# Memory attention with two dense stages on one core: exp(phi) kept row-major, the first batch's keys and values in wide products, tokens left in permuted order

## The chip, the cores and the metric

The kernel runs on one core of a Trainium2 chip. The metric is the device time of one execution in microseconds. Engines are named as in the profile: PE is TensorE's matmul stream, PEld its weight loads, DVE VectorE, ACT ScalarE, POOL GpSimd, SP the engine whose queue issues the loads and stores.

## The reference

Attention runs through 32 memory slots per head (4 batches, 8 heads, 576 tokens, width 64). Its output, 2304 tokens by 512, goes through a leaky two-matrix stage and then through four experts that are mixed by normalised probabilities.

```python
a = np.exp(phi - np.max(phi, axis=2, keepdims=True))
a = a / (np.sum(a, axis=2, keepdims=True) + 1e-09)
k_m = np.einsum('bhsm,bhsd->bhmd', a, k)
v_m = np.einsum('bhsm,bhsd->bhmd', a, v)
scores = scale * np.matmul(q, k_m.transpose(0, 1, 3, 2))
attn = softmax(scores)                       # over the 32 slots
x = rows(np.matmul(attn, v_m))               # (2304, 512)
h = x @ w_in;  x = np.maximum(0.01 * h, h) @ w_out      # w_in, w_out are float64
p = domain_probs / domain_probs.sum(-1, keepdims=True)
out = sum(p[:, e:e+1] * (np.maximum(x @ w1[e], 0) @ w2[e]) for e in range(4))
```

Here axis 2 of phi is the sequence: the maximum and the sum run over the 576 tokens of a head.

## The kernel before, in words

**Layout.** A load of q, k, v or phi of one batch puts two heads on the 128 partitions, 64 partitions to a head; a partition holds nine consecutive rows (tokens) of its head, and four such pairs of heads lie side by side. So token number s is row s mod 9 of partition s // 9. `LT` is 9, `HG` is 4, `NGB` is 2.

**Attention of one batch** (`att_batch`), in its stages: the maximum over the rows in a partition (line 510), a transpose, the maximum over partitions (515), a broadcast back (517, 520), the subtraction (522) and exp (525), all in place in `pl`; a transpose of q in 32x32 blocks (528, `qT`); z, the sums of exp(phi), by matmuls with `ones` (540); the products of exp(phi) with k and v (548), in tiles of 64 by 32 of the array; division by z (574, in `kv`); transposes of the keys to `kb` and the values to `vt` (590, 586); then for each half s of the sequence the scores (610), a block transpose (618), softmax (625 to 638), another transpose (641) and a split of the result into a rounded and a rest part (332, 335: `ah`, `al`). The scores read `qT` in token order, so that neighbouring columns of the moving operand lie 64 elements apart. In batch 0 the k product and the v product are separate, in the other batches they are one.

**First dense stage** (`y_pair`, `moe1_step`). A step is for one batch, half and chunk of 128 hidden units; batch 0 comes first, its first half with chunks 0 to 5, then its second half. A step has six products that make the hidden units (884) and four groups of three that multiply by w_out (951, 952, 953); y pairs (900) put v_m and w_in together. The float64 weights come as pieces of raw words that ACT, DVE and POOL convert (782 to 803); four early pieces use the room of `X2` and `X3`, where q and k of batch 1 are to go. A load into `X1` (v of batch 1) and those pieces lie interleaved in the same stretch of memory.

**What sets the order.** Every operation is handed to a planner (`Plan.op`) with an engine, a cost, a due time and the keys that it reads and writes; `Plan.issue` lists them by cost and due time and so fixes the order on each engine before anything runs. The engines then run in that order, each waiting for what it needs. In the first 50 us of its own reckoning the planner also puts in idle matmuls (line 453) where PE would have nothing to do. The DMA queue of SP is in order as well: a load that has to wait holds up all loads behind it, and a load waits for the landing of the one eight before it.

Of the kernel before, what the change touches and what calls it, by code (L numbers as in the profile page):

```python
# [31 lines left out]
class Plan:  # L32
# [13 lines left out]
    WARM, PART, IDLE, SHORT = (3.0, 50.0), 0.5, 0.22, 0.5  # L46
# [129 lines left out]
def kernel(  # L176
# [42 lines left out]
    PERIOD, LEAD, EACH, LAST = 32.0, 34.0, 3.0, -7.0  # L219
# [150 lines left out]

    def load_probs(t):
        nc.sync.dma_start(out=pr[:, t, :], in_=moe2_domain_probs[t * P:(t + 1) * P, :])
# [71 lines left out]
    def tile_(shape):  # L444
        n = 1
        for size in shape:
            n *= size
        return place("att", new("att", n), *shape)
    ident = tile_([P])

    def idle(bank):

        nc.tensor.matmul(psum[:, bank, 0:P], lhsT=ident, rhs=ident, start=True, stop=True)  # L453
# [3 lines left out]
    pl = [tile_([HG, LT * M]) for i in range(2)]  # L457
    mr = tile_([P])
# [28 lines left out]
    def load(what, b, due):  # L487

        if what == "p":
            plan.op("SP", 1.8, due, lambda: nc.sync.dma_start(  # L490
                out=pl[b % 2], in_=phi[b].rearrange("h s m -> (h s m)").rearrange("(h p w) -> p h w", h=HG, p=P)),
                writes=[f"pl{b % 2}"])
            return
        src, name = {"k": k, "v": v, "q": q}[what], HOME[what][b]
        plan.op("SP", 3.5, due, lambda: nc.sync.dma_start(
            out=home(name), in_=src[b].rearrange("h s d -> (h s d)").rearrange("(h p w) -> p h w", h=HG, p=P)),
            writes=[name])

    def att_batch(b):


        a = pl[b % 2].rearrange("p h (r m) -> p h r m", r=LT)
        nmx, rz = [small[nm][b % 2] for nm in ("nmx", "rz")]
        qn = HOME["q"][b]
        ka = f"pl{b % 2}"
# [4 lines left out]
        op("DVE", 1.25, due, lambda: nc.vector.tensor_reduce(  # L510
            out=mr.rearrange("p (h m) -> p h m", h=HG), in_=a.rearrange("p h r m -> p h m r"), axis=AX.X, op=ALU.max),
           [ka], ["mr"])
        pm = Banks(psum, 1)
        op("PE", 0.13, due, lambda: nc.tensor.transpose(pm[0:P], mr, ident), ["mr", "ident"], [pm])
# [5 lines left out]
        op("PE", 0.13, due, lambda: nc.tensor.transpose(pb[0:P], mb.rearrange("p g t -> p (g t)"), ident),  # L520
           ["mb", "ident"], [pb])
        op("DVE", 1.3, due, lambda: nc.vector.tensor_tensor(
            out=a, in0=a, in1=pb[0:P].rearrange("p (h m) -> p h m", h=HG).unsqueeze(2).to_broadcast([P, HG, LT, M]),
            op=ALU.subtract), [pb], [ka])
        op("ACT", 1.2, due, lambda: nc.scalar.activation(out=pl[b % 2], in_=pl[b % 2], func=AF.Exp), [], [ka])
# [5 lines left out]
        for names in (("k",), ("v",)) if b == 0 else (("k", "v"),):  # L531
            due = yield
            pkv = Banks(psum, 2)
# [3 lines left out]
            def fn(pkv=pkv, src=src, n=len(names), first="k" in names):  # L537
                for r in range(LT * first):
                    for h in range(HG):
                        nc.tensor.matmul(  # L540
                            pkv[2 * D:2 * D + NGB][h * M:(h + 1) * M], lhsT=a[:, h, r], rhs=ones,
                            start=(r == 0), stop=(r == LT - 1),
                        )
                for r in range(LT):
                    for h in range(HG):
                        for g in range(NGB):
                            gs = slice(g * D, (g + 1) * D)
                            nc.tensor.matmul(  # L548
                                pkv[g * 512:g * 512 + n * D][h * M:(h + 1) * M].rearrange("p (i d) -> p i d", i=n),
                                lhsT=a[gs, h, r],  # L550
                                rhs=src[gs, :, h, r * D:(r + 1) * D],
                                start=(r == 0),
                                stop=(r == LT - 1),
                            )
            op("PE", 0.9 + 0.6 * len(names), due, fn, [ka, "ones"] + [HOME[nm][b] for nm in names], [pkv])

            def fn(pkv=pkv):
                nc.vector.tensor_scalar_add(rz, pkv[2 * D:2 * D + NGB], 1e-9)
                nc.vector.reciprocal(rz, rz)
# [3 lines left out]
            for g in range(NGB):  # L563

                def fn(e, g=g, pkv=pkv, n=len(names), lo=lo):
                    for i in range(n):
                        if n == 2 and lo:
                            out, in_ = kv[:, g, 1 - i], pkv[g * 512 + i * D:g * 512 + (i + 1) * D]
                        elif i:
                            break  # L570
                        else:
                            out, in_ = kv[:, g, lo:lo + n].rearrange("p i d -> p (i d)"), pkv[g * 512:g * 512 + n * D]
                        if e == "ACT":
                            nc.scalar.mul(out, in_, rz[:, g:g + 1])
                        else:
                            nc.vector.tensor_scalar_mul(out, in_, rz[:, g:g + 1])
                op("ACT", 0.3, due, fn, [pkv, f"rz{b % 2}"], [f"kv{g}{nm}" for nm in names], also=("DVE", 0.3))

            for nm in names:
# [12 lines left out]
                op("PE", 0.16 * n, due, fn, [f"kv{g}{nm}" for g in range(NGB)] + ["ident"], [pk])  # L592
# [7 lines left out]
        for s in range(2):  # L600
# [16 lines left out]
            op("PE", 0.9, due, fn, ["qT", "kb"], [ps], [f"at{s}"])  # L617
# [36 lines left out]
        ("q", 0): ["q2"], ("v", 0): ["p2", "v1"],  # L654
        ("k", 1): ["p3", "k2", "v2"],
        ("q", 2): ["q3"], ("k", 2): ["k3", "v3"],
# [12 lines left out]
    loads(["p0", "k0", "v0", "q0", "p1", "k1", "q1"])  # L669
# [17 lines left out]
    for t_ in range(NTILE):  # L687
        plan.op("SP", 0.6, 150.0 + 4 * t_, partial(load_probs, t_), [], ["probs"])
# [10 lines left out]
    def raw_piece(src, due, after, alone=False):  # L699
# [18 lines left out]
        plan.op("SP", 0.8 * size / 512, due - FETCH, partial(nc.sync.dma_start, out=t, in_=src), after, [rk])  # L718
# [391 lines left out]
    def second_products(t, n):  # L1110
# [4 lines left out]
        for i in range(2 * TPB):  # L1115
# [80 lines left out]
```

## Time and profile before

| what | us |
|---|---|
| median of 3 runs (lowest, highest) | 1178.17 (1177.49, 1180.21) |
| the profiled execution | 1179.85 |
| its span, first to last instruction | 1177.9 |
| PE busy in the span | 1146.6 |
| DVE, ACT, POOL busy | 681.9, 436.0, 98.9 |

The profile is of one execution. A busy PE isn't PE at its peak, and the clock that TensorE was granted stands beside it in the page. The span and the execution's time differ by what lies around the first and the last instruction.

### The profile page before, as it was taken

What the parts mean: (1) busy time and instruction counts of PE and PEld (TensorE: products, weight loads), DVE (VectorE), ACT (ScalarE), POOL (GpSimd) and SP (SyncE); (2) the same over time, 40 slices, a digit from 0 to 9 for tenths busy, and PEclk for the clock granted to TensorE, in tenths of its full rate; (3) what the DMA queues carried; (4) which work ended last, traced back from release to release, by engine and by line L of the source; (5) the groups of instructions that cost most, each with busy time, mean ns of one, the idle gap of its engine ahead of it and who ended that gap; (6) DMA issues with size and microseconds to landing.
All of it is one profiled execution on the core that took longest, in us unless ns stands there. A gap on an engine that the chain in (4) does not pass through costs nothing.

```text
span 1177.9 us, 18878 instructions
## 1 busy us (share of the span) xinstructions
PE 1146.6 (97%) x7852; PEld 1033.5 (88%) x7852; DVE 681.9 (58%) x1238; ACT 436.0 (37%) x889; POOL 98.9 (8%) x101
## 2 busy tenths in 40 slices
PE   6689999999999999999999999999999999999998
PEld 5468789999999999899989899999999899999997
DVE  3568546863343778767676753445476654454643
ACT  2555437853343544433332421322224123222220
POOL 1352104530000000000000000000000000000000
PEclk8879999999999999999999999999999999999999
DMA  8471302410000228554553563444444644444401
GB/s 322 158 252 44 96 2 89 150 69 1 1 19 1 98 91 318 180 188 187 197 197 143 171 204 144 161 161 161 159 143 139 193 144 161 161 161 161 146 34 53
DMA packets 55957, 160.88 MB, mean 137 GB/s; under 512 B 5441, under 2 KB 24897, under 8 KB 49729
## 3 DMA queue, kind: packets, MB, share of 16 engines
q1 hardware_dynamic: 51264, 100.97, 24.5%
q0 software_dynamic: 4608, 58.72, 14.1%
q8 instruction: 61, 1.00, 0.3%
q14 instruction: 24, 0.19, 0.0%
HBM read 125.60 MB, written 34.08 MB: 136 GB/s over the span
## 4 chain that ended last, share of the span: by engine, by line
PE 95%; DVE 1%; DMA 1%; issue 1%; ACT 1%; POOL 0%; POOLq 0%; SPq 0%; DVEq 0%
PE psum L1059 30%; PE psum L1129 11%; PE psum L1128 11%; PE psum L1127 11%; PE psum L884 9%; PE psum L951 6%; PE psum L953 6%; PE psum L952 6%; PE psum L610 2%; PE psum L900 1%; PE psum L548 1%; PE psum L453 1%; DMA exact<-in_q_dram 1%; DMA exact<-in_v_dram 0%; DVE exact L794 0%
## 5 line engine op out<-in xcount | busy, mean ns | idle before, releaser
L1068 DVE TENSOR_TENSOR exact<-psum,exact 128x384 f32<-128x384 f32 x336 | 184.1, 556 | 272.1 <-PE psum L1059 270.2
L1075 ACT ACTIVATE rounded<-exact 128x384 fp32r<-128x384 f32 x192 | 100.8, 525 | 284.4 <-DVE exact L1068 282.6
L335 DVE TENSOR_TENSOR rounded<-exact,rounded 128x288 fp32r<-128x288 f32 (+3 forms) x225 | 124.8, 571 | 100.3 <-ACT rounded L332 99.2
L1129 PE MATMUL psum<-late,rounded 128*128 128x512 f32 x384 | 150.7, 392 | 0.0
L1128 PE MATMUL psum<-late,rounded 128*128 128x512 f32 x384 | 150.5, 392 | 0.0
L1127 PE MATMUL psum<-late,rounded 128*128 128x512 f32 x384 | 149.3, 389 | 0.0
L1059 PE MATMUL psum<-rounded 128*128 128x384 f32 x768 | 143.2, 335 | 0.0
L1059 PEld LDWEIGHTS psum<-rounded 128*128 128x128 f32 x768 | 134.7, 188 | 2.4 <-DVE exact L1068 0.3
L884 PE MATMUL psum<-rounded 128*128 128x288 f32 x768 | 125.4, 300 | 2.2 <-DVE rounded L335 2.2
L332 ACT CAST rounded<-exact 128x288 fp32r<-128x288 f32 (+3 forms) x239 | 114.8, 501 | 19.8 <-POOL exact L802 5.8
L951 PE MATMUL psum<-rounded 128*128 128x288 f32 x384 | 116.1, 302 | 6.0 <-POOL rounded L335 5.6
L884 PEld LDWEIGHTS psum<-rounded 128*128 128x128 f32 x768 | 110.1, 191 | 9.2 <-issue 5.6
L952 PE MATMUL psum<-rounded 128*128 128x288 f32 x384 | 113.6, 296 | 0.0
L953 PE MATMUL psum<-rounded 128*128 128x288 f32 x384 | 113.6, 296 | 0.0
L1059 PE MATMUL psum<-late,rounded 128*128 128x384 f32 x576 | 109.9, 336 | 0.0
L1079 DVE SCALAR_TENSOR_TENSOR rounded<-exact,rounded 128x384 fp32r<-128x384 f32 x192 | 98.8, 551 | 13.0 <-ACT rounded L1075 13.0
L1059 PEld LDWEIGHTS psum<-late,rounded 128*128 128x128 f32 x576 | 102.0, 188 | 4.0 <-ACT exact L1090 0.2
L939 ACT ACTIVATE exact<-psum 128x288 f32<-128x288 f32 x128 | 53.4, 417 | 137.5 <-PE psum L884 134.6
L1090 ACT COPY exact<-psum 128x384 f32<-128x384 f32 x48 | 23.0, 480 | 198.1 <-PE psum L1059 198.1
L951 PEld LDWEIGHTS psum<-rounded 128*128 128x128 f32 x384 | 72.8, 190 | 18.7 <-issue 10.7
L1129 PEld LDWEIGHTS psum<-late,rounded 128*128 128x128 f32 x384 | 72.0, 188 | 15.1
L1128 PEld LDWEIGHTS psum<-late,rounded 128*128 128x128 f32 x384 | 72.0, 188 | 13.4
(103 smaller groups left out, 1696.1 us busy)
## 6 DMA issues: line engine op xcount, KB each, us to landing
rounded<-kept POOLq DMA_DIRECT2D x22, 1792.0 KB, 7.6
exact<-in_moe_w_dram SPq DMA_DIRECT2D x64, 512.0 KB, 5.0
kept<-rounded SPq DMA_DIRECT2D x10, 1792.0 KB, 6.7
w<-kept POOLq DMA_DIRECT2D x10, 1792.0 KB, 7.6
kept<-w SPq DMA_DIRECT2D x6, 1792.0 KB, 6.4
exact<-in_moe_w_in_dram SPq DMA_DIRECT2D x16, 512.0 KB, 5.5
exact<-in_moe_w_out_dram SPq DMA_DIRECT2D x16, 512.0 KB, 3.5
exact<-in_k_dram SPq DMA_DIRECT2D x4, 1152.0 KB, 6.3
```

Of the source, the lines that this page charges most:

```text
L332: nc.scalar.copy(out, in_) if e == "ACT" else engine(e).tensor_copy(out, in_)
L335: engine(e).tensor_tensor(out=out, in0=in0, in1=in1, op=ALU.subtract)
L884: nc.tensor.matmul(ps, lhsT=l, rhs=r, start=start and n == 0, stop=stop and n == len(seq) - 1)
L951: nc.tensor.matmul(po, lhsT=w2l[:, ds_], rhs=th, start=first, stop=False)
L952: nc.tensor.matmul(po, lhsT=w2h[:, ds_], rhs=tl, start=False, stop=False)
L953: nc.tensor.matmul(po, lhsT=w2h[:, ds_], rhs=th, start=False, stop=last)
L1059: nc.tensor.matmul(ps[k][0:TB], lhsT=l, rhs=r, start=(i == 0), stop=(i == 5))
L1068: plan.op("DVE", dve2(TB), at[k], lambda: nc.vector.tensor_tensor(out=o, in0=ps[k][0:TB], in1=other, op=ALU.add), [ps[k], ok, from_], [key])
L1075: plan.op("ACT", act2(TB), at[k], lambda: nc.scalar.activation(out=th, in_=src, func=AF.Relu), [key, *h_from[hs[c, i]]], [keys[0]])
L1127: nc.tensor.matmul(po[0:DM], lhsT=tl, rhs=w2h[:, c], start=(p == 0 and c == 0), stop=False)
L1128: nc.tensor.matmul(po[0:DM], lhsT=th, rhs=w2l[:, c], start=False, stop=False)
L1129: nc.tensor.matmul(po[0:DM], lhsT=th, rhs=w2h[:, c], start=False, stop=(p == NP2 - 1 and c == 1))
```

## The change

The maximum over nine rows becomes a tree of four two-input maxima (into `aT[1]`, then called `tops`). exp writes into a buffer of its own, `a`, in which one row of all eight heads is contiguous; `pl` becomes a single buffer, and phi of the next batch is loaded behind the exp of this one. z is nine matmuls with 128 weight columns instead of 36 with 32. In batch 0 the products with k and with v are 18 matmuls each, with 128 weight columns and 256 moving ones, of which the blocks off the diagonal are not used; DVE divides by z. The scores read `qT` as it lies, so tokens stay in the order row, partition through both dense stages; the probabilities are loaded and the output is stored in that order by `rows_of`, 32 rows to a DMA, so that there are four DMAs where there was one. An idle matmul has 512 columns instead of 128. Costs and due times of the planner are new.

```diff
-    WARM, PART, IDLE, SHORT = (3.0, 50.0), 0.5, 0.22, 0.5
+    WARM, PART, IDLE, SHORT = (9.0, 50.0), 0.5, 0.9, 1.0
...
-    PERIOD, LEAD, EACH, LAST = 32.0, 34.0, 3.0, -7.0
+    PERIOD, LEAD, EACH, LAST = 32.0, 34.0, 4.0, -7.0
...
+    def rows_of(dram, at):
+        b, at = divmod(at, S)
+        half, at = divmod(at, HB)
+        lo = b * S + half * HB
+        return dram[lo:lo + HB, :].rearrange("(t r) w -> r t w", r=LT)[at // M]
     def load_probs(t):
-        nc.sync.dma_start(out=pr[:, t, :], in_=moe2_domain_probs[t * P:(t + 1) * P, :])
+        for i in range(0, P, M):
+            nc.sync.dma_start(out=pr[i:i + M, t, :], in_=rows_of(moe2_domain_probs, t * P + i))
...
-        op("DVE", 1.25, due, lambda: nc.vector.tensor_reduce(
-            out=mr.rearrange("p (h m) -> p h m", h=HG), in_=a.rearrange("p h r m -> p h m r"), axis=AX.X, op=ALU.max),
+            half = [tops[:, 0:HG * n * M].rearrange("p (h r m) -> p h r m", h=HG, r=n) for n in (4, 2, 1)]
+            pairs = [(half[0], rows[:, :, 0:4], rows[:, :, 4:8]), (half[1], half[0][:, :, 0:2], half[0][:, :, 2:4]),
+                     (half[2], half[1][:, :, 0:1], half[1][:, :, 1:2]), (half[2], half[2], rows[:, :, 8:9])]
+            for out, in0, in1 in pairs:
+                nc.vector.tensor_tensor(out=out, in0=in0, in1=in1, op=ALU.max)
...
-        op("ACT", 1.2, due, lambda: nc.scalar.activation(out=pl[b % 2], in_=pl[b % 2], func=AF.Exp), [], [ka])
+        op("ACT", 1.2, due, lambda: nc.scalar.activation(out=a.rearrange("p r h m -> p h r m"), in_=rows, func=AF.Exp),
+           ["pl"], ["a"])
...
-                    for h in range(HG):
-                        nc.tensor.matmul(
-                            pkv[2 * D:2 * D + NGB][h * M:(h + 1) * M], lhsT=a[:, h, r], rhs=ones,
+                    nc.tensor.matmul(pkv[zat:zat + NGB], lhsT=a[:, r].rearrange("p h m -> p (h m)"), rhs=ones,
...
+                    if b == 0:
+                        for g in range(NGB):
+                            gs = slice(g * D, (g + 1) * D)
+                            nc.tensor.matmul(
+                                pkv[g * 512:g * 512 + HG * D].rearrange("p (h d) -> p h d", h=HG),
+                                lhsT=a[gs, r].rearrange("p h m -> p (h m)"),
+                                rhs=src[gs, 0, :, r * D:(r + 1) * D],
...
-                                ps[g * 512:g * 512 + HB][h * M:(h + 1) * M].rearrange("p (t r) -> p t r", t=M),
-                                rhs=qT[rs, h, :, e].rearrange("p r t -> p t r"),
+                                ps[g * 512:g * 512 + HB][h * M:(h + 1) * M],
+                                rhs=qT[rs, h, :, e],
...
-                    nc.sync.dma_start(out=out[tt * P:(tt + 1) * P, :].rearrange("n (k w) -> n k w", k=KD), in_=a_)
+                    for i in range(0, P, M):
+                        nc.sync.dma_start(
+                            out=rows_of(out, tt * P + i).rearrange("n (k w) -> n k w", k=KD), in_=a_[i:i + M])
```

PE in batch 0, from the z sums on, before (540 is z, 548 the k and then the v product, 590 and 586 the transposes, 610 the scores, 453 idle matmuls):

```order
L540 MATMUL psum<-att 32x2 x36
L548 MATMUL psum<-exact,att 32x64 x72
L453 MATMUL psum<-att 128x128 x3
L590 MATMUL psum<-att,exact 32x128 x8
L453 MATMUL psum<-att 128x128 x8
L610 MATMUL psum<-att,exact 32x288 x16
L548 MATMUL psum<-exact,att 32x64 x72
L610 MATMUL psum<-att,exact 32x288 x16
L586 MATMUL psum<-att,exact 64x128 x2
```

The same place in the changed program (557 z, 563 the k and the v product, 625 and 621 the transposes, 645 the scores, 461 an idle matmul, 935 a y pair):

```order
L557 MATMUL psum<-att 128x2 x9
L563 MATMUL psum<-exact,att 128x256 x18
L461 MATMUL psum<-att 128x512
L563 MATMUL psum<-exact,att 128x256 x18
L625 MATMUL psum<-att,exact 32x128 x8
L645 MATMUL psum<-att,exact 32x288 x16
L621 MATMUL psum<-att,exact 64x128 x2
L645 MATMUL psum<-att,exact 32x288 x16
L935 MATMUL psum<-w_63,exact 32x256 x8
```

The v product (the second 548, the second 563) has moved from between the two score groups to ahead of the key transposes, and the value transposes (586, 621) from behind the second score group to between the two.

DVE at the end of the first half's softmax in batch 0, before (638 and 641 end the softmax, 803 and 794 convert weight pieces):

```order
L638 TENSOR_TENSOR att<-att 128x18x32
L641 STREAM_TRANSPOSE att<-att 128x576
L803 TENSOR_SCALAR exact<-exact 128x512
L803 TENSOR_SCALAR w_63<-w_63 128x2x256
L335 TENSOR_TENSOR rounded<-att,rounded 128x2x288
L794 SCALAR_TENSOR_TENSOR exact<-exact 128x512
L335 TENSOR_TENSOR rounded<-psum,rounded 128x512
L794 SCALAR_TENSOR_TENSOR exact<-exact 128x2x256
```

And in the changed program (653 to 676 are the softmax, 829 is what 794 was, 838 what 803 was):

```order
L662 TENSOR_TENSOR att<-att 128x18x32
L829 SCALAR_TENSOR_TENSOR exact<-exact 128x2x256
L667 TENSOR_REDUCE att<-att 128x18
L669 RECIPROCAL att<-att 128x18
L673 TENSOR_TENSOR att<-att 128x18x32
L676 STREAM_TRANSPOSE att<-att 128x576
L335 TENSOR_TENSOR rounded<-psum,rounded 128x512
L335 TENSOR_TENSOR rounded<-att,rounded 128x2x288
L838 TENSOR_SCALAR w_63<-w_63 128x2x256
L829 SCALAR_TENSOR_TENSOR exact<-exact 128x2x256
L653 STREAM_TRANSPOSE att<-psum 128x18x32
```

The first conversion of a piece in `X2` (128x2x256) has moved from behind the softmax to inside it. The second one follows at the end, and the second half's 653 now stands behind it; the second half's 618 stood ahead of all the rows shown of before.

SP's queue from the ninth load on, before (501 and 490 are phi, 495 and 506 q, k and v, 151 the weight pieces):

```order
L490 DMA att<-in_phi_dram 128x4x288
L151 DMA exact<-in_moe_w_out_dram 128x1024
L495 DMA exact<-in_v_dram 128x4x576
L495 DMA exact<-in_q_dram 128x4x576
L490 DMA att<-in_phi_dram 128x4x288
L495 DMA att<-in_q_dram 128x4x576
L495 DMA exact<-in_k_dram 128x4x576
```

And in the changed program (380 are the probabilities):

```order
L151 DMA exact<-in_moe_w_out_dram 128x1024
L501 DMA att<-in_phi_dram 128x4x288
L506 DMA exact<-in_v_dram 128x4x576
L506 DMA att<-in_q_dram 128x4x576
L506 DMA exact<-in_q_dram 128x4x576
L380 DMA exact<-in_moe_domain_probs_dram 32x4 x8
L506 DMA exact<-in_k_dram 128x4x576
```

The weight piece stands now ahead of phi, q of batch 2 goes ahead of q of batch 1, and eight small loads of probabilities stand ahead of k of batch 1.

## Rows read from the trace of the kernel before

**Rows 1.** The page's slices of the span: PE busy tenths and granted clock.

```profile
PE   6689999999999999999999999999999999999998
PEclk8879999999999999999999999999999999999999
```

**Rows 2.** Windows: busy us (instructions) by engine, then granted clock, DMA share, GB/s.

```profile
40.00:60.00 20.00, 10.68 (x71) 8.72 (x69) 9.88 (x15) 8.80 (x20) 8.66 (x6) 0.83 0.67 233
120.00:1178.00 1058.00, 1053.03 (x6457) 957.69 (x6441) 609.18 (x1144) 381.72 (x782) 61.49 (x64) 1.00 0.37 130
```

**Rows 3.** The chain that ended last, first 61 us: start, us, what.

```profile
13.39 4.41 issue
...
42.19 5.29 DMA exact<-in_v_dram
...
49.38 6.62 DMA exact<-in_q_dram
...
60.24 0.40 PE psum L951
```

**Rows 4.** Timeline of PE: start, us, engine, line, instructions.

```profile
26.83 1.67 PE L548 MATMUL psum<-exact,att 64*32 64x64 f32 x144
33.39 3.17 PE L453 MATMUL psum<-att 128*128 128x128 f32 x26
97.00 1.09 PE L900 MATMUL psum<-w,exact 64*32 64x512 f32 x16
115.45 0.78 PE L540 MATMUL psum<-att 128*32 128x2 f32 x72
119.41 1.06 PE L548 MATMUL psum<-exact,att 64*32 64x128 f32 x52 [1.69 <-issue]
124.90 2.77 PE L610 MATMUL psum<-att,exact 32*32 32x288 f32 x32
```

**Rows 5.** Timeline of the other engines and PE in batch 0's attention.

```profile
4.75 2.09 DVE L510 TENSOR_REDUCE att<-att 128x128 f32<-128x1152 f32 x1 [4.75 <-DMA att<-in_phi_dram]
9.91 1.16 ACT L525 ACTIVATE att<-att 128x1152 f32<-128x1152 f32 x1 [3.83 <-DVE att L522]
27.07 0.78 DVE L618 STREAM_TRANSPOSE att<-psum 128x576 f32<-128x576 f32 x1 [4.80 <-PE psum L610]
32.54 0.69 ACT L630 ACTIVATE att<-att 128x576 f32<-128x576 f32 x1
38.79 1.82 PE L884 MATMUL psum<-rounded 128*128 128x288 f32 x12 [2.23 <-DVE rounded L335]
40.23 1.79 DVE L794 SCALAR_TENSOR_TENSOR exact<-exact 128x512 uint32<-128x512 uint32 x1
```

**Rows 6.** Timeline, 47 to 85 us: conversions, exp of batch 1, its scores.

```profile
47.51 0.69 DVE L794 SCALAR_TENSOR_TENSOR exact<-exact 128x512 uint32<-128x512 uint32 x1 [2.26 <-DMA exact<-in_v_dram]
60.15 1.53 POOL L802 TENSOR_TENSOR exact<-exact 128x512 uint32<-128x512 uint32 x1
61.88 1.92 DVE L794 SCALAR_TENSOR_TENSOR exact<-exact 128x512 uint32<-128x512 uint32 x1
70.01 1.16 ACT L525 ACTIVATE att<-att 128x1152 f32<-128x1152 f32 x1
84.67 2.87 PE L610 MATMUL psum<-att,exact 32*32 32x288 f32 x32
```

**Rows 7.** Windows, columns as in rows 2: behind the exp of batch 1.

```profile
71.20:81.20 10.00, 9.23 (x230) 8.34 (x231) 4.79 (x11) 5.30 (x13) 3.88 (x3) 0.50 0.80 248
```

**Rows 8.** SP's queue: a load of q, loads of probabilities, the last six stores.

```profile
104.00 0.38 SPq L495 DMA_DIRECT2D att<-in_q_dram  x1
104.43 2.03 SPq L372 DMA_DIRECT2D exact<-in_moe_domain_probs_dram  x4
120.97 7.41 SPq L372 DMA_DIRECT2D exact<-in_moe_domain_probs_dram  x10
1167.30 7.33 SPq L1146 DMA_DIRECT2D out_dram<-exact  x6
```

More of the change, by code (lines that the diff above doesn't have):

```diff
@@ L451, in idle @@
     def idle(bank):
-        nc.tensor.matmul(psum[:, bank, 0:P], lhsT=ident, rhs=ident, start=True, stop=True)
+        nc.tensor.matmul(
+            psum[:, bank].rearrange("p (a n) -> p a n", a=4), lhsT=ident,
+            rhs=ident.unsqueeze(1).to_broadcast([P, 4, P]), start=True, stop=True,
+        )
     NR = S // M
-    pl = [tile_([HG, LT * M]) for i in range(2)]
-    mr = tile_([P])
+    pl = tile_([HG, LT * M])
+    a = tile_([LT, HG, M])
     mb = tile_([NGB, D])
@@ L489, in load @@
         if what == "p":
-            plan.op("SP", 1.8, due, lambda: nc.sync.dma_start(
-                out=pl[b % 2], in_=phi[b].rearrange("h s m -> (h s m)").rearrange("(h p w) -> p h w", h=HG, p=P)),
-                writes=[f"pl{b % 2}"])
+            plan.op("SP", 2.7 if b == 0 else 1.5, due, lambda: nc.sync.dma_start(
+                out=pl, in_=phi[b].rearrange("h s m -> (h s m)").rearrange("(h p w) -> p h w", h=HG, p=P)),
+                writes=["pl"])
             return
         src, name = {"k": k, "v": v, "q": q}[what], HOME[what][b]
-        plan.op("SP", 3.5, due, lambda: nc.sync.dma_start(
+        plan.op("SP", 3.0, due, lambda: nc.sync.dma_start(
             out=home(name), in_=src[b].rearrange("h s d -> (h s d)").rearrange("(h p w) -> p h w", h=HG, p=P)),
@@ L519, in att_batch @@
         pb = Banks(psum, 1)
-        op("PE", 0.13, due, lambda: nc.tensor.transpose(pb[0:P], mb.rearrange("p g t -> p (g t)"), ident),
+        op("PE", 0.3, due, lambda: nc.tensor.transpose(pb[0:P], mb.rearrange("p g t -> p (g t)"), ident),
            ["mb", "ident"], [pb])
-        op("DVE", 1.3, due, lambda: nc.vector.tensor_tensor(
-            out=a, in0=a, in1=pb[0:P].rearrange("p (h m) -> p h m", h=HG).unsqueeze(2).to_broadcast([P, HG, LT, M]),
-            op=ALU.subtract), [pb], [ka])
-        op("ACT", 1.2, due, lambda: nc.scalar.activation(out=pl[b % 2], in_=pl[b % 2], func=AF.Exp), [], [ka])
+        op("DVE", 1.35, due, lambda: nc.vector.tensor_tensor(
+            out=rows, in0=rows, in1=pb[0:P].rearrange("p (h m) -> p h m", h=HG).unsqueeze(2).to_broadcast([P, HG, LT, M]),
+            op=ALU.subtract), [pb], ["pl"])
+        op("ACT", 1.2, due, lambda: nc.scalar.activation(out=a.rearrange("p r h m -> p h r m"), in_=rows, func=AF.Exp),
+           ["pl"], ["a"])
         due = yield
@@ L554, in fn @@
                             )
-            op("PE", 0.9 + 0.6 * len(names), due, fn, [ka, "ones"] + [HOME[nm][b] for nm in names], [pkv])
+            op("PE", 2.6, due, fn, ["a", "ones"] + [HOME[nm][b] for nm in names], [pkv])
             def fn(pkv=pkv):
-                nc.vector.tensor_scalar_add(rz, pkv[2 * D:2 * D + NGB], 1e-9)
+                nc.vector.tensor_scalar_add(rz, pkv[zat:zat + NGB], 1e-9)
                 nc.vector.reciprocal(rz, rz)
@@ L562, in att_batch, with fn @@
             lo = "kv".index(sorted(names, key=lambda nm: HOME[nm][b])[0])
-            for g in range(NGB):
+            if b == 0:
+                def fn(pkv=pkv, lo=lo):
+                    for h in range(HG):
+                        hs = slice(h * M, (h + 1) * M)
+                        in_ = pkv[0:1024].rearrange("p (g n) -> p g n", g=NGB)[hs, :, h * D:(h + 1) * D]
+                        nc.vector.tensor_tensor(out=kv[hs, :, lo], in0=in_, in1=rz[hs].unsqueeze(2).to_broadcast([M, NGB, D]),
+                                                op=ALU.mult)
+                op("DVE", 1.0, due, fn, [pkv, "rz0"], [f"kv{g}{nm}" for g in range(NGB) for nm in names])
+            for g in range(NGB * (b > 0)):
                 def fn(e, g=g, pkv=pkv, n=len(names), lo=lo):
@@ L591, in fn @@
                                              lhsT=kv[:, w // 2, 0, e * M:(e + 1) * M], rhs=ident, start=True, stop=True)
[L592 removed]
+                op("PE", 0.3 * n, due, fn, [f"kv{g}{nm}" for g in range(NGB)] + ["ident"], [pk])
                 dst = kb.rearrange("p e m -> p (e m)") if nm == "k" else vt[:, b].rearrange("p h m -> p (h m)")
@@ L668, in loads @@
             load(name[0], b, LOADS[b] + 0.1 * "pqvk".index(name[0]) - 200.0 * (name in ("p0", "k0")))
-    loads(["p0", "k0", "v0", "q0", "p1", "k1", "q1"])
+    loads(["p0", "k0", "v0", "q0", "k1", "q1"])
     for b in range(B):
@@ L717, in raw_piece @@
             t = t.bitcast(U32)
-        plan.op("SP", 0.8 * size / 512, due - FETCH, partial(nc.sync.dma_start, out=t, in_=src), after, [rk])
+        plan.op("SP", 0.7 * size / 512, due - FETCH, partial(nc.sync.dma_start, out=t, in_=src), after, [rk])
         return t, rk
```

32 lines of the change are left out of this document (19 added, 13 removed).

## The prediction

> **What bounds the kernel now.** I read the page's slices first, then windows over stretches, then the chain of waits, then the timelines of the engines and SP's queue in the stretches that this left. In the slices PE is idle for a noticeable share only in the first tenth, and the clock is below full in the same place alone [rows 1]. The windows put a number on it: from 120 us to the end PE is busy for 1053.03 of 1058 us at full clock, so there only PE's own work counts. Between 40 and 60 us it is busy for 10.68 of 20 [rows 2]. A saving can therefore come from two places: PE work that is taken out where PE is full, and a start in which PE gets to its full stretch sooner. A loss can come from added PE work and from the end, where nothing runs beside the last stores.
>
> The chain says what the start waits for: 4.41 us of "issue" at 13.39, then the load of v of batch 1 (42.19, 5.29 us), then that of q (49.38, 6.62 us), and PE goes on with step 1's w_out products at 60.24 [rows 3]. The two loads go into places that early weight pieces hold until they are converted: the load of v starts when the DVE conversion at 40.23 (1.79 us) has ended [rows 5], and that of q some 2 us after v has landed, since the next conversion (47.51) waits for v [rows 6].
>
> **Scores (PE work in the full stretch).** The timeline shows 32 instructions of 288 columns in 2.77 us. They are spread over eight tiles of the array (two pairs of heads by four heads) that run side by side, so each tile works through four of them, 1152 columns, at 2.4 ns a column. The y pairs, which read neighbouring columns, take 1.09 us for 16 instructions of 512 columns, two to each of eight tiles, 1024 columns: 1.06 ns each [rows 4]. At that rate the scores of one batch take 1.23 us, 1.5 less. The bounds are 0 (the stride isn't what makes them slow) and 1.55. I take 1.5, since form and clock are otherwise alike. It applies to two halves in each of batches 1 to 3; a batch's row of 32 instructions is one half, so six of them: **-9.0**.
>
> **z (PE work in the full stretch).** The row has 72 instructions, 36 matmuls, in .78 us. Nine matmuls (18 instructions) with 128 weight columns follow. The nearest row above is that of idle matmuls with 128 weight columns, .122 us each at full clock (3.17 for 26) [rows 4]; 18 of those are 2.2. Below, it stays .78. The moving side is only two columns wide, so weight loading is the work, and I lean to the upper end: 1.9, so +1.1 for a batch, +2.2 for batches 2 and 3.
>
> **k and v of batches 2 and 3.** The tiles are as before. The row has a stall of 1.69 us named issue ahead of them [rows 4]; fewer instructions ahead may shorten it: -1.2 for both together (0 to -1.9).
>
> **The start, batch 0.** Four maxima replace one reduction of 2.09 us [rows 5]: 1152 elements in all, I estimate 1.6 in place of 2.09 from the .69 us that a two-input operation of 512 elements takes [rows 6]. The .4 is not kept: exp now has a weight conversion ahead of it on ACT's queue, so exp stays near 10 to 11.
>
> Each of the two products now has 18 instructions for each half of the partitions (each matmul of the program shows as two in the trace): 18 x 256 columns at 1.06 ns are 4.9 us, if the halves run side by side, and 9.8 at 1.2 GHz. In tiles, the v product's 144 instructions took 1.67 us [rows 4]. This is the dear part of the change. Against it stands the 4.41 us of issue at 13.39 [rows 3], in the middle of the old k product, with no work and no semaphore behind it; I read it as PE's queue of instructions running dry. With 18 instead of 72 matmuls and 9 instead of 36 for z, I expect it to go. The k product ends near 18.5 either way (16.5 to 25, by gap and clock).
>
> The Trainium skill weighs in on both. Its page "Runtime: NRT & Kernel Launch", section "Instruction fetch mechanics", says that fetching is mostly hidden; by that the gap would have another cause and stay, and the start would come 4.4 us later than I say. The trace shows a gap with nothing else to end it, so I keep to the row. The page "TensorEngine Tiling (Array Packing)", section "Theoretical Speedup", speaks against wide products: small tiles should be up to four times as quick. By it a product would take 4 x 1.67, an estimate of 6.7 us where I count 4.9, so 3.6 more for the two; the trace of before has no wide product, and this leans to the first rival.
>
> Behind the products the order helps. The v product now stands ahead of the scores, and the first half's scores end near 26.6, against 27.07 for the start of L618 before. Its exp came only at 32.54 [rows 5], behind copies that waited for the second half's scores; now it follows after three DVE operations of some .8 each, near 30. Step 0's first products come at 34.4 in place of 38.79. The conversion that frees v's place now stands inside the softmax, ahead of 667, and ends near 31 rather than 42.02; with ACT's and POOL's part the load of v starts at 32.3, 9.9 sooner. Queued behind that conversion are the rest of the softmax and the split that step 0 needs (the 34.4 holds it). The load of v has q of batch 2 beside it, so it takes between 5.29 and 6.62 us [rows 3] and lands near 38.5. A conversion and a POOL addition later, at 40.7, q of batch 1 starts (before 49.38) and lands near 46.5 to 47. Before, step 1's products came 4.24 behind its landing (56.00 to 60.24); so now near 51.
>
> Behind that I expect less than 9 us to last. DVE operations on two inputs wait for POOL: the conversion takes 1.92 at 61.88 beside POOL's 1.53, and .69 alone [rows 6]. More of them now fall together, so exp of batch 1 comes at 64 to 65.5 in place of 70.01, and z, which stands on PE behind products of step 2, near 68.6 rather than 71.2: -2.6. PE by then has done some 4.0 us of products more (four groups of three and 18 first products): -4.0. The clock: from 71.2 to 81.2 PE is 9.23 busy at .50 [rows 7], that is 1.2 GHz, behind a stretch in which it stood idle half the time [rows 2]; full speed would give 4.6 of it back. As PE is still idle often, and an idle matmul now asks for a longer gap before it is put in, I take half, -2.3. z of batch 1 adds 1.1. Sum of the start: -2.6 - 4.0 - 2.3 + 1.1, **-8**. Bounds: -1.5, if neither the work nor the clock is won; -16, if exp comes at 61, at its old distance from step 1 (-9.0 in place of -2.6), and the clock is full (-4.6). The scores of batch 1 are among the six.
>
> **Loads of probabilities and other queues.** There are 72 loads in place of 18. In the rows one takes .51 (2.03 for four) to .74 (7.41 for ten) [rows 8]; eight stand ahead of the load of k of batch 1, 4 to 6 us behind the issue of q at 40.7 and its wait for earlier landings. It would start near 54 and land near 60, and is needed near 69 at z: hidden, with 9 us to spare. If the cover is gone, what exceeds it delays batch 1's attention one for one. The others delay weight pieces that arrive well ahead.
>
> **The end.** 24 stores in place of six at the end. The six take 7.33 us, 1.22 each [rows 8]; I take this as the pace of the engines that finish the tiles, since a load is issued in .38 and one of probabilities in .51. Below, four small ones fit into each 1.22 and nothing is added. At .51 each they end at 1167.3 + 12.2, 4.9 later than 1174.6; at .38, 9.1 us, 1.8 later. A small store moves whole rows as the load of q does, so I take **+1.8** (0 to 4.9). The 48 earlier ones are hidden by PE's full stretch.
>
> **Sum.** -8 - 9.0 + 2.2 - 1.2 + 1.8 = -14.2. The profiled execution took 1179.85, so 1165.6; the median of the runs is 1.7 lower, so **1164**.
>
> **The rivals.**
> First: the start doesn't move. PE is cold in it, the wide products run at 1.2 GHz (9.8 us each), and what the queue gains is spent there. For it: the clock at .50 [rows 7] and PE's idle share [rows 2]; against it: the load of v hangs on DVE, not on the second product. Then -9.0 + 2.2 - 1.2 + 1.8 and -1.5 from the start, -7.9: 1170 (1167 to 1174). Nearly the same comes out if the 4.41 us of issue stay where they are: -14.2 + 4.4, 1168.
> Second: the start gives its full -16, with the clock at full and DVE undisturbed: -22.2 (-25 with no loss at the end and the stalls gone), 1154. For it: the load of v moves 9.9 us; against it: POOL beside DVE [rows 6].
> Third: the scores don't get faster, since 32 weight columns and not the stride set their time: 1164 + 9 = 1173. Against it: the y pairs have the same 32 weight columns and 1.06 ns a column.
> Fourth, slower: the last stores. If 1.22 us is SP's own price of a store and not the tiles' pace, 24 of them end at 1167.3 + 29.3, 22.0 us behind 1174.6 [rows 8], where the rest gives 16.0: +6, 1184. With x us for each it outweighs the rest from 24x - 7.3 = 16.0 on, x = .97. For it: nothing in the row tells the two apart; against it: .38 to .74 for each load.
>
> **How the numbers follow.** Forecast (1157 to 1169) .50; first rival .22; second .18; third .05; fourth .05. From 1151 to 1173 lies all but 2 in 10: out of it fall the fourth, half of the third and the tails of the first two. Within 0.2%, 2.4 us, a measurement of this kernel can't be told from no change. Faster has the first four cases almost whole: .90; same .04; slower .06.
>
> **What the profile after would show.** Right: score groups near 1.2 us for 32 instructions; no issue gap of microseconds at 13 to 18; wide products of 4.9 us; the load of v near 32, step 1's w_out products near 51; the clock of the first three slices up. Wrong: wide products near 9 us; the load of v waiting for its piece beyond 36; exp of batch 1 near 70; stores that go on for over 10 us after PE's last matmul.

## The result, and the profile after

The changed kernel takes 1163.37 us (median, 1162.79 to 1163.56) beside 1179.19 of the kernel before in the same set: a ratio of 0.9866, interval 0.9848 to 0.9883, so 15.8 us less. In a later set it took 1164.25 beside 1180.01 (0.9865). The forecast was 1164, within 1151 to 1173. The span went from 1177.9 to 1161.4.

The page's slices of the changed kernel, which answer to [rows 1]: the first tenth still holds the only idle time, and the first and the third slice have gained clock.

```profile
PE   6699999999999999999999999999999999999997
PEclk9889999999999999999999999999999999999999
```

PE's timeline, against [rows 4 to 6]: 557 is z, 563 and 574 the products with k and v, 645 the scores, 919 and 986 a step's first products and its products with w_out.

```profile
11.09 3.97 PE L557 MATMUL psum<-att 128*128 128x2 f32 x18 [1.03 <-ACT att L542]
14.99 7.03 PE L563 MATMUL psum<-exact,att 64*128 64x256 f32 x36
23.01 4.16 PE L563 MATMUL psum<-exact,att 64*128 64x256 f32 x36
28.23 1.24 PE L645 MATMUL psum<-att,exact 32*32 32x288 f32 x32 [0.49 <-ACT exact L332]
37.27 0.40 PE L919 MATMUL psum<-rounded 128*128 128x288 f32 x1 [2.90 <-ACT rounded L332]
54.29 0.61 PE L986 MATMUL psum<-rounded 128*128 128x288 f32 x1 [4.94 <-POOL rounded L335]
69.81 2.07 PE L557 MATMUL psum<-att 128*128 128x2 f32 x18
...
104.38 2.06 PE L557 MATMUL psum<-att 128*128 128x2 f32 x18
106.37 2.25 PE L574 MATMUL psum<-exact,att 64*32 64x128 f32 x144
113.44 1.25 PE L645 MATMUL psum<-att,exact 32*32 32x288 f32 x32
```

Three things are to be seen. The issue gap of 4.41 us is gone, but z and the k product of batch 0 now fill its place: z takes 3.97 where it takes 2.07 in the other batches, the k product 7.03 where the v product, the same work, takes 4.16. The scores take 1.24 to 1.25. And in batch 2, z and the products run from 104.38 to 108.62 with no stall: 4.24 us, where before they took from 115.45 to 120.47, 5.02 [rows 4].

SP's queue and ACT's timeline, against [rows 3, 6, 8]: the loads of v and q of batch 1, exp of batch 1, the last stores.

```profile
35.11 0.37 SPq L506 DMA_DIRECT2D exact<-in_v_dram  x1
42.75 0.37 SPq L506 DMA_DIRECT2D exact<-in_q_dram  x1
65.18 1.17 ACT L542 ACTIVATE att<-att 128x1152 f32<-128x1152 f32 x1
1147.62 11.60 SPq L1182 DMA_DIRECT2D out_dram<-exact  x24
```

v is loaded 7.1 us sooner, q 6.6, exp of batch 1 comes 4.8 sooner. The first of the last stores is issued 19.7 us sooner than at 1167.30, the last issue ends only 15.4 sooner (1159.22 against 1174.63): the end gave 4.3 us back. The span then ends 2.2 us later, where before it took 3.3, so that 16.5 remain.

Windows in which batch 1's z and products fall, columns as in [rows 2]; they answer to [rows 7].

```profile
60.00:70.00 10.00, 9.98 (x69) 8.54 (x69) 8.91 (x13) 5.27 (x10) 4.30 (x4) 0.74 0.75 239
70.00:80.00 10.00, 10.00 (x263) 8.75 (x268) 7.33 (x12) 8.63 (x22) 5.30 (x4) 1.00 0.92 318
```

The stretch that ran at .50 before is at full clock from 70 us on.

### The profile page after: what moved, and what is told of

Read it like the earlier page. It is cut to its first block, busy times and chain, and to the rows that moved or that the text cites. A ratio compares the mean times of both kernels' runs of the same rounds, so it can differ in the third digit from the quotient of the medians.

```text
span 1161.4 us, 17964 instructions
## 1 busy us (share of the span) xinstructions
PE 1132.4 (97%) x7320; PEld 1023.9 (88%) x7320; DVE 688.7 (59%) x1258; ACT 434.6 (37%) x882; POOL 102.7 (9%) x104
## 4 chain that ended last, share of the span: by engine, by line
PE 95%; DVE 2%; DMA 1%; issue 1%; POOL 0%; ACT 0%; SPq 0%; DVEq 0%; POOLq 0%
PE psum L1094 30%; PE psum L1164 11%; PE psum L1163 11%; PE psum L1162 11%; PE psum L919 9%; PE psum L986 6%; PE psum L987 6%; PE psum L988 6%; PE psum L935 1%; PE psum L563 1%; PE psum L557 1%; DVE exact L527 1%; PE psum L645 1%; PE psum L574 1%; DMA exact<-in_v_dram 0%
## 5 line engine op out<-in xcount | busy, mean ns | idle before, releaser
L335 DVE TENSOR_TENSOR rounded<-exact,rounded 128x288 fp32r<-128x288 f32 (+2 forms) x222 | 127.2, 588 | 103.5 <-ACT rounded L332 102.4
```

What stands on the lines that cost most here:

```text
L335: engine(e).tensor_tensor(out=out, in0=in0, in1=in1, op=ALU.subtract)
```

## The experiments

The theory: the gain is that of the scores' stride in PE's full stretch and of an earlier start, which the new order of operations brings; wide z and products cost PE time, and the stores cost at the end. The rivals: the start's gain comes from the wide forms (fewer instructions, no stalls) and not from the order; or from the clock. Times are medians; the changed kernel stands at 1163.4 and 1164.3 in its two sets, 1163.8 in the middle.

**k and v of batch 0 in tiles.**

```diff
-                    if b == 0:
-                        for g in range(NGB):
-                            ... lhsT=a[gs, r] (128 columns), rhs=src[gs, 0, :, ...] (256 columns)
-                        continue
                     for h in range(HG):
```

> The changed kernel, with the k and v products of batch 0 back in tiles of 64 by 32; z, the order and all else stay. In the changed kernel these two wide products take 7.03 and 4.16 us, back to back on the chain. If the wide form is a cost that the start carries to the end: products of 1.7 to 3.4 us each, the load of v of batch 1 some 5 to 7 us sooner than 35.11, and 1157 to 1158 us. If the wide form is what took the 4.4 us gap of issue away: the gap comes back inside the products and the time is 1161 to 1164. If something else (the weight pieces' conversions) covers the products: the products get short, the load of v moves by less than 2 us, and 1162 to 1164.

Measured: 1165.75 (ratio to before 0.9878, 0.9851 to 0.9905), above all three times expected. PE's timeline, then a window:

```profile
15.01 2.28 PE L563 MATMUL psum<-exact,att 64*32 64x64 f32 x144
19.22 0.83 PE L563 MATMUL psum<-exact,att 64*32 64x64 f32 x54
22.09 1.31 PE L563 MATMUL psum<-exact,att 64*32 64x64 f32 x90 [2.04 <-issue]
...
20.00:30.00 10.00, 7.04 (x161) 3.20 (x165) 2.37 (x5) 3.41 (x7) 1.41 (x1) 0.64 0.83 302
```

The k product is 4.75 us shorter, and nothing of it is left: a stall of issue returns inside the v product, and the clock of 20 to 30 us falls to .64, where the changed kernel had 1.00. The load of v starts at 35.02 against 35.11. So the wide form is worth about what it costs in this order; beside the kernel before of their own sets the two can't be told apart (.9878 and .9866).

**z in 36 matmuls.**

```diff
-                    nc.tensor.matmul(pkv[zat:zat + NGB], lhsT=a[:, r].rearrange("p h m -> p (h m)"), rhs=ones, ...)
+                    for h in range(HG):
+                        nc.tensor.matmul(pkv[zat:zat + NGB][h * M:(h + 1) * M], lhsT=a[:, r, h], rhs=ones, ...)
```

> The changed kernel, with z in 36 matmuls of 32 weight columns again, in all four batches. The rows have 2.06 us for the wide z of batches 1 to 3 against .78 before, and 3.97 in batch 0. If each is a plain cost: -3.8 for the three, -2.5 or so in batch 0, 1157 to 1159 us. If the added 108 instructions bring stalls of issue back: less than that or a loss, 1161 to 1165, and the rows show the stall behind z.

Measured: 1168.18, 4.4 slower, where a plain cost would have made it 5 quicker; with stalls 1161 to 1165 was expected. PE's timeline in batches 1, 2 and 3, and a window behind the stall of batch 2:

```profile
67.95 0.78 PE L558 MATMUL psum<-att 128*32 128x2 f32 x72
73.61 0.55 PE L575 MATMUL psum<-exact,att 64*32 64x128 f32 x4 [2.23 <-issue]
...
105.94 0.78 PE L558 MATMUL psum<-att 128*32 128x2 f32 x72
110.78 0.42 PE L575 MATMUL psum<-exact,att 64*32 64x128 f32 x7 [1.95 <-issue]
...
148.56 0.66 PE L575 MATMUL psum<-exact,att 64*32 64x128 f32 x28 [0.87 <-issue]
...
110.00:120.00 10.00, 9.22 (x95) 7.50 (x96) 1.87 (x5) 2.07 (x6) 0.00 (x0) 0.83 0.39 120
```

z is as short as it was, but each batch's products stall for 2.23, 1.95 and .87 us near their end, more than the 1.28 that z saves in two of three, and the clock is at .83 behind the second. Up to step 1 this kernel is 2.1 us ahead of the changed one (52.16 against 54.29); by batch 1's scores it is 1.5 behind (79.97 against 78.50). Here, then, nine wide matmuls are the quicker z: behind them the changed kernel has no such stall in any batch.

**The old stride in the scores**, and **the new reading alone** in the kernel before:

```diff
-                                ps[g * 512:g * 512 + HB][h * M:(h + 1) * M],
+                                ps[g * 512:g * 512 + HB][h * M:(h + 1) * M].rearrange("p (t r) -> p t r", t=M),
...
-                                rhs=qT[rs, h, :, e],
+                                rhs=qT[rs, h, :, e].rearrange("p r t -> p t r"),
```

> The changed kernel, with the scores reading the queries with the old stride (tokens come out of them in the old order while loads of probabilities and stores keep the new one, so the output's rows are mixed). If the stride alone made the scores slow: 32 instructions take 2.8 us again where they take 1.0 to 1.25, +10 for batches 1 to 3 and +1 to +3 for batch 0's two on the start, 1174 to 1176 us. If the rest of the change made them quick: 1163 to 1165.

> The kernel before with one edit: the scores read the queries as they lie; tokens then leave them in the new order, while loads of probabilities and stores keep the old one, so that the output's rows are mixed. If the scores are worth the same alone as in the change: six groups from 2.83 to 1.0 to 1.25, -10 in the full stretch, and up to -3 in batch 0: 1167 to 1170 us. If they only pay together with the rest: over 1174.

Measured: 1175.65 with the old stride, 11.8 slower; 1168.35 with the new reading alone (the same edit the other way round in the kernel before), 11.7 quicker than 1180.01. The group of the scores, all eight, in the changed kernel, with the old stride, then in the kernel before as it is and with the new reading (busy us, mean ns of one):

```profile
L645 PE MATMUL psum<-att,exact 32*32 32x288 f32 x256 | 9.4, 414 | 0.5 <-ACT exact L332 0.5
```

```profile
L645 PE MATMUL psum<-att,exact 32*32 32x288 f32 x256 | 21.5, 763 | 0.5 <-ACT exact L332 0.5
```

```profile
L610 PE MATMUL psum<-att,exact 32*32 32x288 f32 x256 | 23.3, 764 | 0.0
```

```profile
L610 PE MATMUL psum<-att,exact 32*32 32x288 f32 x256 | 10.6, 415 | 2.0 <-issue 2.0
```

The stride alone is worth 12.1 us of PE's time (12.7 in the kernel before), and nearly all of it shows in the end. It pays with and without the rest of the change.

**The last stores**: one store to a tile (the rows land in the wrong order), and two of the four issued by ACT for the last six tiles.

```diff
-                    for i in range(0, P, M):
-                        nc.sync.dma_start(out=rows_of(out, tt * P + i)..., in_=a_[i:i + M])
+                    nc.sync.dma_start(out=out[tt * P:(tt + 1) * P, :]..., in_=a_)
...
-                        nc.sync.dma_start(
+                        (nc.scalar if i >= P // 2 and tt >= NTILE - 6 else nc.sync).dma_start(
```

> The changed kernel, with one store of 128 rows to a tile (the rows land in the wrong order). In the changed kernel 24 issues at the end take 11.60 us and end 5.6 us after DVE's last product starts; before, six took 7.33. If issuing them sets the end: 3 to 4 us less, 1159 to 1160.5 us. If the landing of the last data sets it: within 1 us of 1163.4.

> The changed kernel, with two of the four stores of each of the last six tiles issued by ACT, the other two by SP. The changed kernel issues the last 24 at .48 us each, 11.60 in all. If a queue's pace of issuing sets the end: twelve on each fit behind the tiles, 2 to 4 us less, 1159.5 to 1161.5. If DMA or landing sets it: 1163 to 1164.

> The changed kernel once more, beside the others of this set: 1162 to 1165 us.

Measured: 1161.07 and 1161.09; the changed kernel in the second set 1164.25. The two queues of the split version:

```profile
1149.11 7.59 SPq L1182 DMA_DIRECT2D out_dram<-exact  x12
...
1149.12 7.66 ACTq L1182 DMA_DIRECT2D out_dram<-exact  x12
```

Twelve on each queue take 7.6 us, about what six took before, so SP's pace of .48 us for each of 24 stores set the end, at 2.7 to 3.2 us.

**The idle matmuls**: those of before (128 columns, from 3.0 on, for shorter gaps), and none (with the split stores).

```diff
-    WARM, PART, IDLE, SHORT = (9.0, 50.0), 0.5, 0.9, 1.0
+    WARM, PART, IDLE, SHORT = (3.0, 50.0), 0.5, 0.22, 0.5
...
+    WARM, PART, IDLE, SHORT = (9.0, 50.0), 0.0, 0.9, 1.0
```

> The changed kernel with the idle matmuls of before: 128 columns, from 3.0 us of the planner's reckoning on, put in for shorter gaps. In the changed kernel z of batch 0 takes 3.97 us where later ones take 2.06, and the k product 7.03 where the v product behind it takes 4.16: 4.8 us on the chain of the start. If the clock of the start is what these lose, and it reaches the end: the two at 2.1 and 4.2, the load of v of batch 1 near 30.5, 1158 to 1160 us. If the loads of v and q, DVE and POOL take it back up to step 1: 1161 to 1163. If the added instructions bring stalls of issue: slower, over 1164.

> The changed kernel with two queues for the last stores (1161.1 by itself) and no idle matmuls at all. Two of them stand between the k and the v product, 1.05 us on the chain. If they only cost: 1 us less, 1160. If the clock of the start hangs on them: the k and v products and step 0 run at half rate for longer, 1162 to 1166.

Measured: 1164.15, no change; 1162.76, some 1.7 over the split version, but the four times of each overlap. With those of before, batch 0's z and k product, and a window in which they fall; then the k product in the second execution of the changed kernel:

```profile
11.08 2.75 PE L554 MATMUL psum<-att 128*128 128x2 f32 x18 [1.50 <-ACT att L539]
13.77 6.84 PE L560 MATMUL psum<-exact,att 64*128 64x256 f32 x36
...
12.50:19.20 6.70, 6.70 (x33) 5.60 (x34) 2.58 (x1) 2.18 (x3) 1.90 (x2) 0.50 1.05 393
```

```profile
15.07 5.58 PE L563 MATMUL psum<-exact,att 64*128 64x256 f32 x36
```

z gained 1.2 us, the k product next to nothing: idle matmuls ran from 1.38 us on, with gaps of 1.55 and 1.50 us ahead of z, and the granted clock still was .50 from 12.5 to 19.2 us. So these didn't win the 4.8 us of half rate in batch 0. What such a gain would be worth, the changed kernel's second execution shows: its k product took 5.58 us in place of 7.03 and v was loaded at 33.75 in place of 35.11, yet z of batch 1 came at 69.87, against 69.81. The 1.4 us are gone before batch 1's z. With the idle matmuls of before it came at 69.91.

Without idle matmuls the first half's scores come 1.1 us sooner than in the split version (27.36 against 28.50) and z of batch 1 at about the same time (70.11, 70.20); then a stall follows in batch 1's products, and its scores are 2.0 us later (81.29, 79.25):

```profile
76.44 0.42 PE L574 MATMUL psum<-exact,att 64*32 64x128 f32 x8 [2.16 <-issue]
```

The time falls into the range that was expected for a colder start, but what its trace shows is this stall.

**The order**: the same instructions under the costs and due times of before, with wide products and with products in tiles.

```diff
-            op("PE", 2.6, due, fn, ["a", "ones"] + [HOME[nm][b] for nm in names], [pkv])
+            op("PE", 0.9 + 0.6 * len(names), due, fn, ["a", "ones"] + [HOME[nm][b] for nm in names], [pkv])
...
-        op("DVE", 1.8, due, fn, ["pl"], ["aT1"])
+        op("DVE", 1.25, due, fn, ["pl"], ["aT1"])
```

> The changed kernel's instructions in the order that the costs of before give: costs and due times in the planner are those of before, so the v product stands between the scores of batch 0's halves again, and the conversion that frees v's place behind the softmax. If the order brings the start forward: the load of v of batch 1 goes back from 35.1 to 40 or later, step 1's w_out products from 54.3 to 58 to 61, and the time is 1167 to 1171. If the start's gain comes from z and the products alone: 1163 to 1165.

> The changed kernel with the planner's costs and due times of before (1179.2 by themselves) and with the k and v products of batch 0 in tiles again, so that these products, too, take about what those costs say. If the wide products in an order made for short ones are the loss: most of the 15 us comes back, 1165 to 1170 us, the load of v of batch 1 near 40 to 43. If other costs (loads, the long waits of weight pieces) misplace the order: 1174 to 1180.

Measured: 1179.18 with wide products, 15.4 slower, 8 above the range expected, and as slow as the kernel before (ratio 1.0001, 0.999 to 1.0012); 1175.67 in tiles, 9.9 slower than tiles in the new order and in the range that was named for other costs that misplace the order. Timelines of the first: the scores stand between the two products again, v is loaded at 48.51 and exp of batch 1 comes at 80.11.

```profile
15.14 7.11 PE L563 MATMUL psum<-exact,att 64*128 64x256 f32 x36
27.63 1.92 PE L645 MATMUL psum<-att,exact 32*32 32x288 f32 x32 [1.94 <-DVE att L546]
29.48 6.77 PE L563 MATMUL psum<-exact,att 64*128 64x256 f32 x36
...
48.51 0.37 SPq L506 DMA_DIRECT2D exact<-in_v_dram  x1
...
80.11 1.16 ACT L542 ACTIVATE att<-att 128x1152 f32<-128x1152 f32 x1
```

And of the second:

```profile
41.67 0.37 SPq L506 DMA_DIRECT2D exact<-in_v_dram  x1
...
73.12 1.16 ACT L542 ACTIVATE att<-att 128x1152 f32<-128x1152 f32 x1
```

With short products the old order loads v about as early as the kernel before did (42.19); with wide ones it is 6.3 us later than that. So the start's gain isn't there without the new order, and wide products in the old one lose more than that gain. How much of it the order brings by itself isn't shown, since under the old costs this program starts worse than the kernel before (exp of batch 1 at 80.11 and 73.12 against 70.01). Why the tiles under the old costs end 7.3 over the new reading alone (1168.35) isn't wholly settled: the stores are some 3 of it, and exp of batch 1 is 3.1 us later than in the kernel before although v came sooner. Which of the new costs carries the order wasn't tried singly, nor were the tree of maxima, exp's own buffer and the single `pl` undone.

**A mix**: the k product in tiles, the v product wide, with the split stores.

```diff
-                    if b == 0:
+                    if b == 0 and not first:
```

> The changed kernel with two queues for the last stores, and with the k product of batch 0 in tiles of 64 by 32 while the v product stays wide. In tiles the k product took 2.28 us in place of 7.03, and the stall of issue came 54 instructions into a v product in tiles. If the wide v product covers the fetching: no stall in it or in the scores, 4.7 us less on the chain of the start, of which DVE and the loads let 1 to 3 through: 1158 to 1160.5. If the stall only moves (into the scores or step 0) or the clock falls: 1161 to 1164.

Measured: 1160.06 (0.984 of before, 0.9814 to 0.9866), the lowest median of all.

```profile
15.00 2.28 PE L574 MATMUL psum<-exact,att 64*32 64x64 f32 x144
19.21 4.79 PE L563 MATMUL psum<-exact,att 64*128 64x256 f32 x36
...
62.00 1.17 ACT L542 ACTIVATE att<-att 128x1152 f32<-128x1152 f32 x1
72.80 0.41 PE L574 MATMUL psum<-exact,att 64*32 64x128 f32 x4 [0.69 <-issue]
```

No stall stands in batch 0's products or scores, and exp of batch 1 is 3.2 us sooner than in the changed kernel. But a stall of .69 us is back in batch 1's products, and batch 1's scores come only .85 sooner (77.65 against 78.50). At the end about 1 us remains against the split stores alone (1161.09), which these times can't prove: the first of the last stores goes out at 1147.93, against 1149.11 there and 1147.62 in the changed kernel's first profile.

## Why the prediction was right, point by point

**Scores.** Right: 1.24 us against 1.23 forecast. The term of -9 was somewhat short: the six groups of batches 1 to 3 take 6.96 us in place of 16.97, 10.0 less (two back to back in batch 1 take 1.99), and undoing the edit costs 11.8 with batch 0's two.

**z.** The price was right (2.06 against 1.9). It was added as +1.1 for a batch, while the stall in the products behind it stood in a term of its own (-1.2), so that batches 2 and 3 summed to +1.0. Measured from the start of z to the end of the products, the two batches come to nothing: batch 2 takes .78 us less (5.02 to 4.24), and batch 3, which had hardly a stall before, .70 more (3.55 to 4.25). Batch 3 before, then in the changed kernel:

```profile
157.18 0.78 PE L540 MATMUL psum<-att 128*32 128x2 f32 x72
...
159.24 1.49 PE L548 MATMUL psum<-exact,att 64*32 64x128 f32 x82 [0.20 <-issue]
```

```profile
140.83 2.06 PE L557 MATMUL psum<-att 128*128 128x2 f32 x18
142.83 2.25 PE L574 MATMUL psum<-exact,att 64*32 64x128 f32 x144
```

The run with z in 36 matmuls shows that price and stall are one: without the wide z the stalls are 2.23, 1.95 and .87 us, and taking it out of the change costs 4.4.

**Stalls of issue.** Read rightly as PE running out of instructions, but their number is only half of it. In every run that has them, the stalls of the first 200 us end at the same places of PE's stream: after 222 or 223, 350, 476 to 478, 604, 732, 859, 1115, 1371, 1626 or 1882 matmul instructions, each with its weight load, so in steps of some 128 or a multiple. Each of them ends 2.2 to 2.8 us after the start of an instruction packet of 16 KB, and the page of before has 61 such packets (queue q8) for 15704 instructions of PE, one for some 257. PE's busy time with its count of matmul instructions up to the end of a stall, before, with z in 36 matmuls, and without idle matmuls; then the queue from 74.1 to 75.1 us in the last of these, whose stall ends at 76.44:

```profile
0.00:17.79 17.79, 8.50 (x223) 0.97 0.93 341
```

```profile
0.00:73.60 73.60, 50.95 (x604) 0.84 0.73 253
```

```profile
0.00:76.43 76.43, 45.84 (x476) 0.84 0.70 244
...
q8 instruction: 1, 0.02, 6.0%
```

What counts is how fast PE gets through one such stretch of 128. In these three runs and the mix, eight of the nine stalls stand behind a stretch that ran in 1.6 to 2.2 us (the ninth, in batch 1 before, behind one of 3.57); the shortest of the changed kernel takes 2.41, with six matmuls of the wide z beside 121 short ones, and has no stall. Fewer instructions alone don't rule a stall out: without idle matmuls and in the mix a stretch falls on short ones alone, in spite of the same wide z, and stalls of 2.16 and .69 us follow. The Trainium skill's page "Runtime: NRT & Kernel Launch", section "Instruction fetch mechanics", says that fetching is mostly hidden. That doesn't hold here where matmuls are short: the stalls take .20 to 4.41 us.

**The start's steps.** The mechanism was right, 2 to 3.5 us late from the k product to step 1, and 1.2 by z of batch 1: the k product's end at 22.0 (18.5 forecast), the first half's scores at 29.5 (26.6), step 0 at 37.3 (34.4), v loaded at 35.1 (32.3), q at 42.75 (40.7), step 1 at 54.3 (51), exp of batch 1 at 65.2 (64 to 65.5), z at 69.8 (68.6). The mis-sized step is batch 0's z and k product: the working took the rate of rows at full speed, 4.9 for the product, and gave z no place at all; they took 7.03 and 3.97. The start came out right all the same, since the clock behind it did better than half: 70 to 80 us ran at 1.00 against .56 for the same window before, where only half of the loss was counted as won. With the scores and z taken off the 19.7 us by which the first of the last stores moved, some 9.6 are the start's, against 8. Two slips in the working don't touch the sum: the first rival's terms come to -7.7 and not -7.9, and POOL's 1.53 us in [rows 6] ended at 61.68, ahead of the conversion at 61.88; beside that stood POOL's next operations, 3.31 us from 61.62 on.

**The cause of the start's gain.** The prediction put it on the order (the v product ahead of the scores, the conversion inside the softmax). The runs under the old costs bear that out so far that without the new order v goes from 35.1 back to 41.7 (tiles) or 48.5 (wide), and 9.9 or 15.4 us are lost; they don't show which step of the order counts. What it didn't see is how much of the change hangs on this: it priced wide products as dear and the order as a gain, but not that the first would ruin the old order.

**Wide products.** The Trainium skill's page "TensorEngine Tiling (Array Packing)", section "Theoretical Speedup", spoke for tiles, up to four times as quick. The trace shows 4.16 wide against 1.67 in tiles [rows 4], 2.5 times. Yet the tiles gave nothing in the changed kernel: with both products in tiles a stall of 2.04 us and a clock of .64 stand where the time was won.

**The end.** The mechanism was right, the size low: .48 us for an issue, not .38, so 4.3 us lost by issuing and 3.2 in the span, against 1.8. The bound of .51 held.

**The sum.** -14.2 against -16.5 in the span: the scores gave 10.0 and not 9.0, z with its stalls .1 less and not 1.0 more, the start some 9.6 and not 8, and the end took back 3.2 and not 1.8. That the median lies only .6 us from the forecast is partly luck: beside it the kernel before ran at 1179.19, 1.0 above the median that the forecast started from. The start's -8 is luck in part, too: a product and a z that were priced too low, and a clock that was priced too low as a gain.

## What to carry to other kernels

Where a stage is made of many short matmuls, price it with the stall that it can run into: fewer and longer instructions can win though each row says they are dearer. Where the stall falls depends on how many instructions PE has had up to there, so an edit in one stage can bring it back in another. When an operation's duration changes, the order that a planner made from its old duration is part of the change; try the new work in the old order before crediting the work. Splitting a transfer multiplies its issues: at the end of a program, where nothing runs beside them, spread them over two queues.

## What the runs showed of the hardware

Batch 0's z and most of its k product run at half the rate that the same shapes have later, while the granted clock of that window is given as 1.00:

```profile
10.00:20.00 10.00, 8.97 (x43) 7.93 (x44) 5.47 (x5) 4.67 (x6) 2.58 (x2) 1.00 1.05 392
```

The 1.00 is no reading there: the trace of the changed kernel holds no entry of the clock before 20.86 us, and the column counts a stretch without an entry as full. With the idle matmuls of before the entries start sooner, and the same product stands at .50, the 1.2 GHz level, up to 19.24 us. Full clock is on record from 20.86 us on in the changed kernel's first execution and from 18.00 in its second; in all three PE had been busy without a gap since 11.1 to 11.2 us. At the v product's rate (4.16 us for 36, so .116 each) behind these times and at half of it ahead of them, the k product comes to 7.1, 6.9 and 5.6 us, an estimate; 7.03, 6.84 and 5.58 were measured. So in the first 20 us the durations of known shapes tell the rate where the clock column can't. Why the rise came at 18.0 in one execution and at 20.9 in another wasn't settled.
